# Batch 2 alone in the first MLP, its heads with values side by side, and two steps planned later

## The chip, the cores and the metric

One core of a Trainium2 chip runs the whole program in one launch. The metric is the device time of one execution in microseconds, from several timed runs; one more execution was profiled. TensorE does the matmuls, VectorE and ScalarE the elementwise work, GpSimd a little of it, and SyncE starts most of the transfers. The profile calls them PE, DVE, ACT, POOL and SP, and weight loads of TensorE PEld.

## The reference

Three stages run one behind the other on 4 batches of 448 tokens, all in float32 (weights come as float64):

```
attn = softmax(cap * tanh(q @ k.T / (8 * cap))) @ v     # 12 heads of 64, 448 tokens, per batch
x    = attn, heads side by side                         # (448, 768) per batch
xn   = (x - mean) / sqrt(var + 1e-6) * g_ln
x    = x + relu(xn @ w_ch1) @ w_ch2                     # first MLP, hidden 3072
u    = x + (relu(x.T @ w_tok1) @ w_tok2).T              # tokens mixed, hidden 256
out  = u + relu(u @ w_ch1') @ w_ch2'                    # second MLP, hidden 1536
```

## The kernel before

Activations lie transposed: 768 channels as 6 blocks of 128 partitions, 448 tokens along the free axis. A product of the MLPs is split in high and low parts of float32 and takes three passes (high by high, low by high, high by low), so a hidden block is 18 matmuls of 448 columns (L587) and an output block, over a group of four hidden blocks, 12 (L608). The first MLP has 6 such groups, the second 3. Each group is 4 + 6 weight tiles; a tile is converted from float64 the first time (`piece`, L269, on ScalarE and VectorE), stored split in DRAM (`kept`), and loaded from there in every later use (L296). There are three tile buffers (`split`).

The batches are staged. Batches 0 and 1 do their attention first, in early heads with float32 matmuls (L363, L384). Batch 0 then does one group of the first MLP alone, batches 0 and 1 do five groups as a pair (each tile serves both), batch 1 makes up its first group while batch 0 mixes tokens, and so on through the second MLP. Batches 2 and 3 follow in the same manner. Their heads are laid into the stream of the first two batches: scores from split operands (L366), tanh and exp on ScalarE (L369, L370), maxima on VectorE (L374), the split of the exponentials (L394, L396 to L400), and the values.

There are two ways to do the values of such a head. The usual one (L411 to L414) keeps 96 + 64 weight columns, the high part of v with 32 columns of ones beside it, which give the sums, and the low part. It takes 11 matmuls for a head, and the last block of tokens uses 64 rows for one of them. The other, for batches in `BESIDE` (L62, L406 to L409), puts high and low part of v side by side in 128 columns: 7 matmuls for a head, but no sums. VectorE then sums the exponentials itself (L421, two instructions of 896 columns), adds two small instructions (L425, L426), and the two halves of the result are joined through ScalarE (L429) and VectorE (L430).

Nothing is issued in the order of the code. `add` records steps with a key, their engines, and what they read and write. `emit` (L121) then plays the steps through a model with a cost for each engine and a shared port of VectorE and GpSimd ("+" in an engine's name), takes of the steps that are ready the one with the lowest key, and writes the instructions in that order. Each engine executes its own queue in order. Steps of heads and norms on TensorE get a key lowered by `URGENT` (1000), so they go as soon as the model has them ready. The keys come from numbers such as `T_ATT2` and `PACE2` (L68): batch 2's heads start at key 171.18, one for every 25.

`N_AHEAD` groups of weights are converted ahead of the first MLP, beside the early heads (L717). `normalise` (L534) takes a buffer of its own for each of six blocks (`centred`, of which four are the buffers `own` for the heads' exponentials).

Of the kernel before, what the change touches and what calls it, by code (L numbers as in the profile page):

```python
# [15 lines left out]
ALU = mybir.AluOpType  # L16
# [42 lines left out]

URGENT, SCORES, PREPARE, LOAD = 1000.0, 19.31, 4.58, 24.58  # L60

BESIDE = (3,)  # L62

N0, N1, N20, N2 = 1, 3, 1, 2
T_LN0, T_LN1 = 7.69, -20.0
T_AHEAD, N_AHEAD, AHEAD_PACE = 14.0, 1, 5.0
T_ALONE, STRETCH0, T_PAIR, STRETCH1 = 85.0, 1.3, 165.0, 1.14
T_ATT2, PACE2, T_ATT3, PACE3 = 171.18, 25.0, 500.0, 40.0  # L68
LEAD, RAW_AHEAD, EVACUATE, TOKENS_AHEAD = 6.3, 9.57, -7.49, 17.25


# [15 lines left out]
class Program:  # L87
# [33 lines left out]
    def emit(self):  # L121
# [10 lines left out]
        for _ in self.steps:  # L132
            t, e = min((max(free[e], min(s.ready for s in q)), e) for e, q in queue.items() if q)
            step = min((s for s in queue[e] if s.ready <= t), key=lambda s: s.key)
            for other in step.engines:
                queue[other].remove(step)
            step.run(e) if step.flexible else step.run()
            if e in step.port:
                t = port = max(t, port) + step.engines[e]
            else:  # L140
                t += step.engines[e]
            free[e] = end = t
            end += self.LATER.get(e, 0.0)
            for s in step.users:
                s.ready = max(s.ready, end + (0.2 if e not in s.engines else 0.0 if e == "pe" else 0.13))
                s.waits -= 1
                if not s.waits:
                    enter(s)
# [3 lines left out]
def block_kernel(ctx: ExitStack, tc: tile.TileContext, qkv, cap, gln, w1, w2, wt1, wt2, con, out):  # L152
# [111 lines left out]


    raws, wholes = ring(RAW), ring(WHOLE)
    kept = {}

    def piece(src, m, target, to):  # L269

# [6 lines left out]
        add("act", m, lambda: act(lo, lo.bitcast(U32), AF.Copy, scale=2.0 ** -29), (), [r])  # L277
        add("dve+", m // 2, lambda: dve.tensor_scalar(f, f, 3, None, op0=ALU.logical_shift_left), (), [w])  # L278
        add("dve+", m, lambda: dve.scalar_tensor_tensor(f, hi, -(1 << 31), f, op0=ALU.bitwise_and, op1=ALU.bitwise_or), [r], [w])  # L279
        add("dve+", m, lambda: dve.tensor_tensor(f, f, lo, op=ALU.add), [r], [w])  # L280
        g = f.bitcast(F32)
        add("act/dve*+", m, lambda e: copy(e, target[:, 0], g), [w], to)
        add("dve+", m, lambda e: low(engine_of[e], target[:, 1], g, target[:, 0]), [w], to)

    def load(no, w, row, cols):

# [247 lines left out]
    def normalise(b):  # L534
        rstd = RSTD[0]
        eng = LN_ENGINES[b]
        for e in range(NCC):
            o, g = centred[e], BIG[b % 2][e]
            if b >= 2:
                subtract(b, e, o)  # L540
            add("dve+", S, lambda o=o, e=e: dve.scalar_tensor_tensor(
# [172 lines left out]
    with tc.manual_schedule():  # L714
        setup()
        prog.key = T_AHEAD
        for g in range(N_AHEAD):  # L717
            prepare(g)
        prog.key = 0.0
        attention(0, 0.0, 3.97)  # L720
        prog.key += T_LN0
# [75 lines left out]
```

## Time and profile before

| | |
|---|---|
| median of 3 runs | 1398.46 us (1396.95 to 1399.26) |
| profiled execution | 1399.07 us, span 1397.3 us |
| TensorE busy | 1370.9 us, 98% of the span, 6512 matmuls |
| VectorE busy | 887.7 us, 64% |
| ScalarE busy | 612.0 us, 44% |
| GpSimd busy | 63.2 us, 5% |
| chain that ended last | PE 89%, DVE 6%, ACT 3%, DMA 1% |
| mean granted clock of TensorE | 0.995 |

A row of the windows has, behind the stretch and its length, the busy time of PE, PEld, DVE, ACT and POOL with their instructions in brackets, then the granted clock, the mean share of the transfer engines, and GB/s. A row of a timeline has start and time of an instruction or of several alike; the end of a matmul is modelled, and matmuls overlap, so the step from one start to the next tells what one costs. The times of one engine's instructions can overlap a little too. In the order of instructions below, a row is one instruction of an engine's queue, or several alike (x3), with what it writes and reads.

### The profile page before, as it was taken

Reading aid. Unit: us, or ns where it says so; the run is one execution under the profiler, and the core shown is the slowest. Engines: PE = TensorE matmul, PEld = TensorE weight load, DVE = VectorE, ACT = ScalarE, POOL = GpSimd, SP = SyncE. Lnnn points to the kernel's source line nnn. Section 1 sums busy time; section 2 is a strip of 40 time slices with the busy share of each in tenths; the row PEclk is TensorE's granted clock in tenths of the full one; section 3 lists DMA queues with packets and bytes.
Section 4 is the critical chain, followed back from the end, with each engine's and each line's share of the span. In section 5 each row is a group of like instructions: output and inputs, shape, how many; then the busy total and the mean of one; then the engine's idle time right before and its main releaser. Section 6 shows DMA issues by size and latency. Waiting matters only on the chain.

```text
span 1397.3 us, 17773 instructions
## 1 busy us (share of the span) xinstructions
PE 1370.9 (98%) x6512; PEld 1178.4 (84%) x6512; DVE 887.7 (64%) x1602; ACT 612.0 (44%) x995; POOL 63.2 (5%) x52
## 2 busy tenths in 40 slices
PE   8999989999999999999999999999999999999998
PEld 3335578889898999988999999999999999999997
DVE  5999698988898899999989973212122232232221
ACT  7986567675657656776656421010100111111000
POOL 0000002010011001100010000000000000000000
PEclk9999999999999999999999999999999999999999
DMA  8885447667675756467565576643232456554366
GB/s 264 275 268 161 142 123 244 226 203 227 196 229 191 240 177 223 156 218 235 192 202 195 178 232 200 208 149 128 84 122 93 148 166 189 186 168 151 124 197 194
DMA packets 135671, 262.16 MB, mean 188 GB/s; under 512 B 10144, under 2 KB 72864, under 8 KB 135584
## 3 DMA queue, kind: packets, MB, share of 16 engines
q1 hardware_dynamic: 135008, 260.74, 57.9%
q8 instruction: 51, 0.84, 0.2%
q10 hardware_dynamic: 576, 0.29, 0.1%
q14 instruction: 36, 0.29, 0.1%
HBM read 198.86 MB, written 62.13 MB: 187 GB/s over the span
## 4 chain that ended last, share of the span: by engine, by line
PE 89%; DVE 6%; ACT 3%; DMA 1%; issue 1%; SPq 0%; ACTq 0%; DVEq 0%
PE bank L587 37%; PE bank L608 37%; PE sc L366 3%; PE bank L384 3%; PE bank L682 2%; PE bank L663 2%; PE bank L408 1%; PE sc L363 1%; DVE m L374 1%; ACT x L369 1%; PE bank L414 1%; PE bank L413 1%; PE bank L466 1%; ACT x L370 1%; PE bank L639 1%
## 5 line engine op out<-in xcount | busy, mean ns | idle before, releaser
L608 PE MATMUL bank<-h,split 128*128 128x448 f32 x2592 | 547.9, 367 | 3.4 <-DVE x L612 2.9
L587 PE MATMUL bank<-big,split 128*128 128x448 f32 x2592 | 548.1, 368 | 3.0 <-ACT big L543 2.0
L587 PEld LDWEIGHTS bank<-big,split 128*128 128x128 f32 x2592 | 485.9, 188 | 48.2 <-ACT big L543 3.3
L608 PEld LDWEIGHTS bank<-h,split 128*128 128x128 f32 x2592 | 484.9, 188 | 46.7 <-DVE x L612 3.6
L592 ACT ACTIVATE h<-bank 128x448 fp32r<-128x448 f32 x144 | 78.3, 544 | 398.1 <-PE bank L587 397.6
L612 DVE TENSOR_TENSOR x<-x,bank 128x448 f32<-128x448 f32 x216 | 133.4, 619 | 186.1 <-PE bank L608 184.0
L593 DVE SCALAR_TENSOR_TENSOR h<-bank,h 128x448 fp32r<-128x448 f32 x144 | 89.3, 621 | 183.9 <-ACT h L592 183.3
L276 ACT ACTIVATE whole<-raw 128x384 f32<-128x384 f32 (+2 forms) x130 | 77.6, 600 | 45.4 <-DVE split L172 42.0
L280 DVE CUSTOM_DVE_ANT_0 whole<-raw,whole 128x768 uint16<-128x768 uint16 (+2 forms) x130 | 85.6, 659 | 0.6
L172 DVE TENSOR_TENSOR split<-whole,split 128x384 fp32r<-128x384 f32 (+1 forms) x126 | 79.2, 632 | 4.3 <-ACT split L176 3.6
L279 DVE SCALAR_TENSOR_TENSOR whole<-raw,whole 128x384 int32<-128x384 int32 (+2 forms) x130 | 81.3, 627 | 0.2
L277 ACT ACTIVATE raw<-raw 128x384 int32<-128x384 uint32 (+2 forms) x130 | 77.6, 600 | 0.0
L176 ACT ACTIVATE split<-whole 128x384 fp32r<-128x384 f32 (+1 forms) x85 | 47.9, 564 | 43.6 <-PE bank L608 19.7
L172 POOL TENSOR_TENSOR ks<-area,ks 64x512 fp32r<-64x512 f32 x23 | 31.7, 1377 | 675.5 <-ACT ks L347 675.5
L374 DVE TRANSPOSE_TENSOR_REDUCE m<-x 128x28 f32<-128x896 f32 x48 | 52.5, 1101 | 8.2 <-ACT x L370 7.7
L278 DVE TENSOR_SCALAR whole<-whole 128x384 int32<-128x384 int32 (+2 forms) x130 | 53.7, 416 | 2.3 <-ACT whole L276 1.9
L374 DVE TRANSPOSE_TENSOR_REDUCE m<-area 128x28 f32<-128x896 f32 x48 | 52.9, 1102 | 0.8 <-ACT area L370 0.8
L369 ACT ACTIVATE area<-sc,tsc 128x896 f32<-128x896 f32 x48 | 48.2, 1005 | 11.1 <-DVE el L400 6.3
L370 ACT ACTIVATE area<-area,cap_t 128x896 f32<-128x896 f32 x48 | 49.9, 1040 | 0.6
L369 ACT ACTIVATE x<-sc,tsc 128x896 f32<-128x896 f32 x48 | 46.7, 996 | 6.9 <-DVE tsc L252 4.3
L394 ACT ACTIVATE eh<-area 128x896 fp32r<-128x896 f32 x48 | 45.4, 946 | 9.4 <-PE bank L408 3.5
L370 ACT ACTIVATE x<-x,cap_t 128x896 f32<-128x896 f32 x48 | 49.0, 1037 | 0.3
(117 smaller groups left out, 1116.0 us busy)
## 6 DMA issues: line engine op xcount, KB each, us to landing
split<-kept SPq DMA_DIRECT2D x136, 384.0 KB, 4.1
split<-kept SPq DMA_DIRECT2D x102, 512.0 KB, 3.7
raw<-in_w SPq DMA_DIRECT2D x72, 384.0 KB, 3.5
kept<-split SPq DMA_DIRECT2D x72, 384.0 KB, 3.6
raw<-in_w SPq DMA_DIRECT2D x54, 512.0 KB, 4.0
kept<-split SPq DMA_DIRECT2D x54, 512.0 KB, 3.3
area<-in_qkv SPq DMA_DIRECT2D x38, 480.0 KB, 4.1
area<-in_qkv SPq DMA_DIRECT2D x35, 192.0 KB, 3.3
```

The lines of the kernel that those rows point to most:

```text
L172: eng.tensor_tensor(out, whole, high.bitcast(F32), op=ALU.subtract)
L276: add("act", m, lambda: act(f.bitcast(F32), hi.bitcast(F32), AF.Copy, scale=2.0 ** -112), [r], [w])
L279: add("dve+", m, lambda: dve.scalar_tensor_tensor(f, hi, -(1 << 31), f, op0=ALU.bitwise_and, op1=ALU.bitwise_or), [r], [w])
L280: add("dve+", m, lambda: dve.tensor_tensor(f, f, lo, op=ALU.add), [r], [w])
L369: add("act", 2 * S, lambda e=e, sc=sc: act(e, sc.at[:, :, :S], AF.Tanh, scale=tsc), [sc], eb)
L370: add("act", 2 * S, lambda e=e: act(e, e, AF.Exp, scale=cap_t), (), eb)
L374: add("dve", 2 * S, lambda half=half, e=e: dve.tensor_reduce(m.at[:, half].rearrange("p c j -> p (c j)"), e.rearrange("p c (j i) -> p (c j ...
L587: mm(ph.at[:, :S], w[:, wi, cc * P:(cc + 1) * P], src[cc].at[:, xi], start=(cc, n) == (0, 0), stop=(cc, n) == (NCC - 1, 2))
L592: add("act", S, lambda ht=ht, ph=ph: act(ht.at[:, 0], ph.at[:, :S], AF.Relu), [ph], [ht], early=EVACUATE)
L593: add("dve", S, lambda ht=ht, ph=ph: dve.scalar_tensor_tensor(ht.at[:, 1], ph.at[:, :S], 0.0, ht.at[:, 0].bitcast(F32), op0=ALU.max, op1=A ...
L608: mm(py.at[:, :S], w[:, wi, i * P:(i + 1) * P], h[i].at[:, hi], start=(i, n) == (0, 0), stop=(i, n) == (G - 1, 2))
L612: add("dve", S, lambda x=x, py=py: dve.tensor_tensor(x.at, x.at, py.at[:, :S], op=ALU.add), [py], [x], early=EVACUATE)
```

## The change

`BESIDE` holds batch 2 as well. N1 goes from 3 to 6: batch 2 does all six groups of the first MLP alone, and batch 3 all six alone, beside batch 2's token mixing and behind it; the pair of the two shares only the second MLP. The keys of the heads of batches 2 and 3 are other numbers. In `emit`, a TensorE step with a key below zero (a step of a head or a norm) that reads what another engine wrote is planned 2.0 us later than the model has its input, past 200 us of the model's time. In the group converted ahead, the integer addition and the low part of the split go to GpSimd. `normalise` uses the two buffers `two` in turn for batches 2 and 3.

```diff
-BESIDE = (3,)
-
-N0, N1, N20, N2 = 1, 3, 1, 2
+BESIDE = (2, 3)
+SPARE, SPARE_FROM = 2.0, 200.0
+
+N0, N1, N20, N2 = 1, 6, 1, 2
-T_ATT2, PACE2, T_ATT3, PACE3 = 171.18, 25.0, 500.0, 40.0
+T_ATT2, PACE2, T_ATT3, PACE3 = 230.0, 35.0, 650.0, 25.0
...
             for s in step.users:
-                s.ready = max(s.ready, end + (0.2 if e not in s.engines else 0.0 if e == "pe" else 0.13))
+
+                spare = SPARE if "pe" in s.engines and s.key[0] < 0 and end > SPARE_FROM else 0.0
+                s.ready = max(s.ready, end + (0.2 + spare if e not in s.engines else 0.0 if e == "pe" else 0.13))
...
-    kept = {}
+    kept, ahead = {}, False
...
-        add("dve+", m, lambda: dve.tensor_tensor(f, f, lo, op=ALU.add), [r], [w])
+        add("pool+" if ahead else "dve+", m, lambda e: engine_of[e].tensor_tensor(f, f, lo, op=ALU.add), [r], [w])
...
-        add("dve+", m, lambda e: low(engine_of[e], target[:, 1], g, target[:, 0]), [w], to)
+        add("pool+" if ahead else "dve+", m, lambda e: low(engine_of[e], target[:, 1], g, target[:, 0]), [w], to)
...
-            o, g = centred[e], BIG[b % 2][e]
+            o, g = centred[e] if b < 2 else two[e % 2], BIG[b % 2][e]
...
         prog.key = T_AHEAD
+        ahead = True
         for g in range(N_AHEAD):
             prepare(g)
+        ahead = False
```

The lines of the changed kernel stand three further down in the heads and the MLPs (L411 of the order now is L408 before, L590 is L587, L611 is L608, L534 is L531).

On TensorE, the first head of batch 2 in the kernel before, just behind the second norm (bank_111 takes the head's values, eh, el and vs are its split exponentials and values):

```order
```

The lines of the changed kernel stand three further down in the heads and the MLPs (L411 of the order now is L408 before, L590 is L587, L611 is L608, L534 is L531).

On TensorE, the first half of the first head's values of batch 2 in the kernel before, just behind the second norm (bank_111 takes the head's values; eh, el and vs are its split exponentials and values):

```order
L587 MATMUL bank_112<-big_84,split_77 128x448 x12
L411 MATMUL bank_111<-eh_98,vs_97 96x448
L413 MATMUL bank_111<-eh_98,vs_97 64x448
L414 MATMUL bank_111<-el_99,vs_97 96x448
L411 MATMUL bank_111<-eh_98,vs_97 96x448
L413 MATMUL bank_111<-eh_98,vs_97 64x448
L414 MATMUL bank_111<-el_99,vs_97 96x448
L587 MATMUL bank_112<-big_84,split_77 128x448 x6
```

The same half in the changed kernel:

```order
L590 MATMUL bank_114<-big_85,split_79 128x448 x18
L411 MATMUL bank_111<-eh_98,vs_97 128x448
L411 MATMUL bank_111<-el_99,vs_97 128x448
L411 MATMUL bank_111<-eh_98,vs_97 128x448
L411 MATMUL bank_111<-el_99,vs_97 128x448
L611 MATMUL bank_112<-h_86,split_77 128x448 x3
```

Six matmuls of 96 and 64 columns have become four of 128; of the second half, five have become three. The first of them stands 132 matmuls of products behind the norm's L531, where it stood 30 behind it.

On TensorE, behind the variance of batch 1's norm in the kernel before (L511 the variances, L531 the spread of the factors, big_84 and big_85 the normed input of batches 0 and 1):

```order
L511 MATMUL bank_112<-inv_c,area 112x2 x4
L587 MATMUL bank_113<-big_84,split_79 128x448 x18
L531 MATMUL bank_111<-area,ones 128x448
L587 MATMUL bank_114<-big_85,split_79 128x448 x12
L366 MATMUL sc_115<-qs_95,ks_96 128x448 x4
L587 MATMUL bank_114<-big_85,split_79 128x448 x6
L366 MATMUL sc_116<-qs_95,ks_96 128x448 x4
```

The same place in the changed kernel (L514 is L511, L369 is L366):

```order
L514 MATMUL bank_112<-inv_c,area 112x2 x4
L611 MATMUL bank_114<-h_86,split_78 128x448 x3
L611 MATMUL bank_114<-h_87,split_78 128x448 x3
L611 MATMUL bank_114<-h_88,split_78 128x448 x3
L611 MATMUL bank_114<-h_89,split_78 128x448 x3
L590 MATMUL bank_113<-big_84,split_79 128x448 x12
L534 MATMUL bank_111<-area,ones 128x448
L590 MATMUL bank_113<-big_84,split_79 128x448 x6
L590 MATMUL bank_114<-big_85,split_79 128x448 x12
L369 MATMUL sc_115<-qs_95,ks_96 128x448 x4
L590 MATMUL bank_112<-big_84,split_77 128x448 x12
L590 MATMUL bank_114<-big_85,split_79 128x448 x6
```

An output block of 12 matmuls more stands between the variances and the factors, and 6 of the 18 matmuls on batch 0 now stand behind the factors, ahead of the first on batch 1; further products on batch 0 (bank_112) come forward between those of batch 1.

On VectorE, the first pieces of weights in the kernel before (L374 and L377 are maxima of heads, L433 sums; whole and raw are a piece in conversion, split its result):

```order
L278 TENSOR_SCALAR whole_75<-whole_75 128x384
L279 SCALAR_TENSOR_TENSOR whole_75<-raw_72,whole_75 128x384
L280 ISA whole_75<-raw_72,whole_75 128x768
L374 TENSOR_REDUCE m_100<-x_82 128x28
L433 TENSOR_REDUCE rs_103<-bank_112 32x14
L172 TENSOR_TENSOR split_77<-whole_75,split_77 128x384
L278 TENSOR_SCALAR whole_76<-whole_76 128x384
L374 TENSOR_REDUCE m_100<-x_82 128x28
L279 SCALAR_TENSOR_TENSOR whole_76<-raw_73,whole_76 128x384
L377 TENSOR_REDUCE rm_105<-m_100 128x14
L280 ISA whole_76<-raw_73,whole_76 128x768
L178 CAST split_77<-whole_76 128x384
```

And GpSimd in the changed kernel, where it now has them (L283 is the addition of L280, L175 the low part of L172):

```order
L283 TENSOR_TENSOR whole_75<-whole_75,raw_72 128x384
L175 TENSOR_TENSOR split_77<-whole_75,split_77 128x384
L283 TENSOR_TENSOR whole_76<-whole_76,raw_73 128x384
L175 TENSOR_TENSOR split_77<-whole_76,split_77 128x384
L283 TENSOR_TENSOR whole_75<-whole_75,raw_74 128x384
L283 TENSOR_TENSOR whole_76<-whole_76,raw_72 128x384
L175 TENSOR_TENSOR split_78<-whole_75,split_78 128x384
L175 TENSOR_TENSOR split_78<-whole_76,split_78 128x384
```

Each piece gives an L280 and an L172 to GpSimd, 28 instructions for the 14 pieces of the group; L278, L279 and most copies (L178) stay on VectorE. ScalarE keeps the same two conversions for each piece.

## Rows read from the trace of the kernel before

**Rows 1.** windows: stretch, length, busy us (count) per engine, clock, DMA share, GB/s

```profile
18.00:90.00 72.00, 66.60 (x218) 26.88 (x217) 69.32 (x128) 70.91 (x100) 0.00 (x0) 1.00 0.89 284
90.00:131.00 41.00, 37.98 (x135) 19.09 (x133) 38.11 (x72) 31.59 (x45) 0.00 (x0) 0.93 0.59 187
175.00:200.00 25.00, 20.93 (x91) 16.92 (x90) 23.60 (x52) 15.15 (x27) 0.00 (x0) 0.93 0.28 91
200.00:490.00 290.00, 290.00 (x1411) 258.28 (x1411) 259.86 (x466) 196.49 (x326) 37.05 (x26) 1.00 0.68 218
595.00:665.00 70.00, 65.55 (x332) 59.72 (x331) 66.01 (x129) 47.77 (x90) 4.96 (x4) 0.98 0.68 223
```

**Rows 2.** timeline of TensorE: start, us, line, names; values of a batch 2 head

```profile
296.60 0.36 PE L411 MATMUL bank<-eh,vs 128*96 128x448 f32 x1
...
297.81 0.98 PE L366 MATMUL sc<-qs,ks 128*128 128x448 f32 x4
...
302.27 0.36 PE L411 MATMUL bank<-eh,vs 128*96 128x448 f32 x1
...
303.59 0.77 PE L366 MATMUL sc<-qs,ks 128*128 128x448 f32 x3
```

**Rows 3.** timeline of TensorE: values of a batch 3 head

```profile
681.84 0.36 PE L408 MATMUL bank<-eh,vs 128*128 128x448 f32 x1
...
682.65 1.38 PE L587 MATMUL bank<-big,split 128*128 128x448 f32 x6
...
689.54 0.36 PE L408 MATMUL bank<-eh,vs 128*128 128x448 f32 x1
...
690.15 2.01 PE L587 MATMUL bank<-big,split 128*128 128x448 f32 x9
```

**Rows 4.** groups by line, VectorE, 0 to 122 us: busy, mean ns, idle before

```profile
L280 DVE CUSTOM_DVE_ANT_0 whole<-raw,whole 128x768 uint16<-128x768 uint16 x8 | 4.5, 560 | 0.2
...
L172 DVE TENSOR_TENSOR split<-whole,split 128x384 fp32r<-128x384 f32 x8 | 4.2, 541 | 0.1
L172 DVE TENSOR_TENSOR split<-whole,split 128x512 fp32r<-128x512 f32 x6 | 4.1, 682 | 0.1
...
L280 DVE CUSTOM_DVE_ANT_0 whole<-raw,whole 128x1024 uint16<-128x1024 uint16 x6 | 3.9, 650 | 0.0
```

**Rows 5.** timeline of all engines, 226.5 to 230 us

```profile
227.32 1.87 POOL L172 TENSOR_TENSOR ks<-area,ks 64x512 fp32r<-64x512 f32 x1 [8.31 <-ACT ks L347]
...
227.95 1.79 DVE L280 CUSTOM_DVE_ANT_0 whole<-raw,whole 128x1024 uint16<-128x1024 uint16 x1
```

**Rows 6.** timeline of TensorE behind the second norm

```profile
188.85 0.92 PE L531 MATMUL bank<-area,ones 112*128 112x448 f32 x2
191.74 4.22 PE L587 MATMUL bank<-big,split 128*128 128x448 f32 x11 [1.96 <-ACT big L543]
```

**Rows 7.** waits of TensorE, 200 to 1397 us: us, times, longest

```profile
PE bank L682 <- DVE h L669: 2.1, 1, 2.1
PE bank L608 <- DVE x L612: 1.6, 1, 1.6
PE bank L682 <- ACT h L668: 0.6, 1, 0.6
PE bank L608 <- DMA split<-kept: 0.6, 1, 0.6
PE bank L682 <- DVE h L644: 0.2, 1, 0.2
```

**Rows 8.** groups by line, VectorE, 200 to 800 us

```profile
L374 DVE TRANSPOSE_TENSOR_REDUCE m<-area 128x28 f32<-128x896 f32 x47 | 51.8, 1102 | 0.8 <-ACT area L370 0.8
...
L421 DVE TRANSPOSE_TENSOR_REDUCE n<-area 128x28 f32<-128x896 f32 x24 | 26.3, 1097 | 0.0
```

**Rows 9.** chain of waits: start, us, what

```profile
857.78 14.60 PE bank L587 x72
...
1348.29 14.88 PE bank L608 x72
```

## The prediction

> **What bounds the kernel now.** I read the windows by stage first, then TensorE's timeline at the places that the change touches, then its waits, and last the groups of VectorE. From 200 to 490 us TensorE is busy 290.00 of 290 us at clock 1.00 [rows 1], and that is the picture up to the end but for a few waits: all of them after 200 us make 5.1 us together [rows 7]. So past 200 us the time is the number of matmuls by the step from one to the next, and only fewer or shorter matmuls, or new waits, change it. Before 131 us it is otherwise. Between 18 and 90 us ScalarE is busy 70.91 of 72 us, VectorE 69.32 and TensorE 66.60 [rows 1]: three engines nearly full at once, so relief of one alone is worth little. Two things to keep in mind: none of these waits is a head's step (those are L363 to L414), and VectorE is busy 259.86 of 290 us in the stretch from 200 to 490, 0.90 of it, without costing TensorE anything.
>
> **Values side by side (batch 2).** The row of a start to the row behind the step tells what a half of the values costs. Before, the first half goes from 296.60 to 297.81, 1.21 us for six matmuls, and the second from 302.27 to 303.59, 1.32 us for five, the one of 64 rows being slow to come and to leave [rows 2]. A head of batch 3, which has them side by side already, takes 681.84 to 682.65, 0.81 us, and 689.54 to 690.15, 0.61 us [rows 3]. So 2.53 becomes 1.42: 1.11 us a head, by 12 heads 13.3 us, all of it on an engine that never waits there. Bounds: 13 to 13.6, if the places of the heads make the step behind the 64 rows cheaper or dearer. Term: -13.3.
>
> **What the sums cost VectorE.** Each head gains two L421 of 1.097 us [rows 8], 2.2 us, 26 us over 12 heads; the other exchanges are about even. Against that the new keys spread the heads: from its first scores to its last gathering step (L444) batch 2 lay across 1206 matmuls of products and now lies across 1668. The old 1206 with 12 heads is 1206 x 0.203 + 12 x 4.15 (values and eight scores) = 295 us of TensorE, about the stretch of rows 1, with 264 us of VectorE by its share. The same products now hold 8.7 heads: 1206 x 0.203 + 8.7 x 3.04 = 271 us of TensorE. VectorE gets 8.7 x 2.2 = 19 us more and 3.3 heads less. A head's VectorE work is at least its two L374 of 1.10 us [rows 8]; with the split of the exponentials and values I estimate 6. That leaves 263 us (276 with the lower number), so VectorE would stand at 0.97 (1.02) where it stood at 0.90. Before, 0.90 cost nothing, and the stretch 595 to 665 with 66.01 of 70, 0.94, cost 4.45 us of TensorE [rows 1], though there the tokens wait on VectorE at once. With the main banks to spare I take +3 us, ends 0 and +17 (that rate, 4.45/70, over all 271 us).
>
> **The group converted ahead.** 14 pieces give two VectorE instructions each to GpSimd: 8 x 0.560 + 6 x 0.650 for L280 and 8 x 0.541 + 6 x 0.682 for L172 [rows 4], 16.8 us off VectorE before 90 us. ScalarE loses nothing and is as full; what it has free is 1.1 us up to 90 and 9.4 of the 41 us up to 131. GpSimd's own queue is empty there, 0.00 us busy [rows 1], so nothing of a head stands behind the new work, but GpSimd also holds up VectorE: an L280 that began beside a GpSimd instruction of 1.87 us took 1.79 us and ended just behind it [rows 5], against a mean of 0.650 [rows 4], so a meeting costs up to 1.14 us. Of 128 VectorE instructions in that window 28 go; of the 100 left some 42 (L278, L279, the copies) read as these do. 28 x 0.42 x 1.14 is 13 us given back, and about 3 of relief stay. Ends: 28 x 1.14 = 32 given back, a start 15 us later; none given back, and ScalarE's room, 8 us earlier. I take -3.
>
> The Trainium skill has a rule for this place (SBUF — State Buffer, Who interferes with whom): a VectorE instruction with two SBUF inputs and a GpSimd instruction that reads SBUF take one shared port for the whole instruction, and the second waits. The trace agrees, 1.79 us instead of 0.650 [rows 4, 5]; taken as a full meeting at each of the 28 it would be the later end above, and the second rival goes half the way there.
>
> **Behind the second norm.** The step that spreads the factors starts at 188.85, the next product at 191.74, 1.96 us of it idle for the normed input, and then 11 products take 4.22 us where 2.2 would do [rows 6]; the window's clock is 0.93 [rows 1], so part of the products ran at the lower of the two levels, 1.2 GHz, after that pause. Now 12 more matmuls stand ahead of L531 and six behind it that need nothing new: 1.2 us of the pause is filled for certain, and if it is short enough the clock stays and about 2 us more come back; the first values of a head no longer press in there either. I take -3, between -5 (all of it) and +2 (batch 0's products are spent earlier and are missing later).
>
> **The pace of the products.** 72 products take 14.60 us at 857.78 and 14.88 us at 1348.29 [rows 9], at the same clock: 202.8 and 206.7 ns, two steady paces. In rows 3 the nine behind a second half of side-by-side values run at the slower one (2.01 us are eight steps and a last one of 0.36: 206 each), the six behind a first half at the faster (1.38 us, 204). So side by side in batch 2 should put more products on the slow pace, and batch 3's three groups behind the tokens of batch 2 are at a place like that of 1348.29, where the pair ran like 857.78. I count some 700 products more at 3.9 ns: +2.7 us, ends 0 and +6.
>
> **Edits at nothing.** N1 = 6 leaves the matmuls as they are. It adds 42 loads (24 of 384 KB, 18 of 512 KB), all of kept tiles: a group alone needs 6.3 MB in 29 us, 215 GB/s, with a head's 0.7 MB every 20 us 250; 284 GB/s ran between 18 and 90 us [rows 1]. They go through SyncE's queue behind the same buffers as now; without that cover each late tile would cost 0.6 us, as the one of the weight loads did [rows 7]. Planning heads 2 us later removes no wait, since none there is a head's [rows 7]; it puts the step behind some ten products, and a head has 28 us of TensorE until the next, so its cost is 0, ends -1 and +1. The two norm buffers make each block wait for the one before last, some six times 2.5 us of serial work that VectorE's queue carries among the evacuations behind it (L612), under a group of batch 1's products (144 x 0.203 = 29 us). Mixing tokens of batches 0 and 1 loses the heads beside it, but VectorE gets batch 2's norm there: 0, ends -4 and +4.
>
> **Sum.** -13.3 + 3 - 3 - 3 + 2.7 = -13.6 us on 1399.07, the profiled execution's own time (span 1397.3 and 1.8 around it), gives 1385.5. The median shown is 0.6 us lower, so I say 1385 us.
>
> **Rivals.**
> A, VectorE becomes the bound under batch 2's heads, L612 and L593 come late and TensorE waits for banks. For it: 0.97 by my sum, with everything after it late. Against it: 0.90 to 0.93 cost nothing. It decides from a share of 1.0 on; at the rate of 595 to 665 it is +17, the start and the second norm then give nothing, since what they give is waited for again: -13.3 + 17 + 2.7 = +6.4, 1405 us. Slower.
> B, GpSimd gives back more than it takes and the second norm keeps its pause: start +4 (17 us lost to meetings and 4 more of latency, against 16.8), norm 0, VectorE +3, pace +2.7: -3.6, 1395 us. For it rows 5; against it the many instructions of that stretch that read PSUM or one input and don't meet.
> C, VectorE was the true bound of the first 131 us. Then the start gives 8, the norm 5, and no new wait comes: -13.3 - 8 - 5 + 1 = -25, 1373 us. Against it ScalarE's 70.91 of 72.
> That the change does not do what it says can only be so for the 2 us of spare: with no wait to remove it is idle in every case here.
>
> **How the numbers follow.** The forecast 0.72 (its own range 1379 to 1391), A 0.06, B 0.12, C 0.10. A measurement of this kernel tells 0.2%, 2.8 us, from no change. The forecast, C and most of B are faster by more: 0.92. Within it: 0.04, from B's far end and the near side of A. Slower: 0.04. The range 1376 to 1394 leaves out A, the larger part of C and some of B, less than 2 in 10.
>
> **What would show it.** In the profile after: values of batch 2 as seven L411 of 0.20 us a step, 48 matmuls fewer; TensorE's first main product (L590) some 3 us earlier than L587 had it, and VectorE no longer full between 18 and 90 us; after the second norm a pause under 1 us and a clock of 1.00; VectorE at 0.95 or more from 200 to 490 and short waits on L615 or L596, 3 us in all; products at 14.88 us for 72 in batch 3's last groups alone. I am wrong if TensorE's waits past 200 us pass 15 us, if the first product comes no earlier, or if a head of batch 2 still costs over 2 us of values.

## The result, and the profile after

The changed kernel takes 1381.51 us (median of 4 runs, 1379.37 to 1381.71) against 1398.28 for the kernel before: a ratio of 0.9877, interval 0.986 to 0.9894, 16.8 us faster. I had said 1385, with 1376 to 1394 around it. The profiled execution is one of 1379.37 us with a span of 1377.5, 19.8 below that of before, and the terms below are compared with those 19.8. TensorE has 6464 matmuls, 48 fewer.

The same stretches as in [rows 1]:

```profile
18.00:90.00 72.00, 66.69 (x210) 27.51 (x209) 60.40 (x100) 69.82 (x98) 32.59 (x28) 0.95 0.86 281
90.00:131.00 41.00, 38.23 (x142) 18.35 (x141) 39.74 (x78) 33.18 (x47) 0.00 (x0) 1.00 0.65 202
175.00:200.00 25.00, 21.61 (x105) 18.33 (x104) 23.70 (x56) 15.08 (x30) 0.00 (x0) 1.00 0.38 126
200.00:490.00 290.00, 290.00 (x1428) 267.46 (x1427) 262.31 (x488) 183.26 (x312) 25.29 (x18) 1.00 0.70 226
595.00:665.00 70.00, 69.67 (x346) 62.80 (x345) 65.36 (x136) 39.67 (x73) 0.00 (x0) 1.00 0.59 193
```

VectorE is relieved up to 90 us, as said; from 200 to 490 it stands at 262.31 of 290, 0.905, not at the 0.97 that I had worked out; and the stretch from 595 to 665 has got back 4 of its 4.45 idle us.

The values of a head of batch 2 on TensorE's timeline, where [rows 2] stood:

```profile
284.37 0.36 PE L411 MATMUL bank<-eh,vs 128*128 128x448 f32 x1
...
285.18 0.98 PE L369 MATMUL sc<-qs,ks 128*128 128x448 f32 x4
...
292.07 0.36 PE L411 MATMUL bank<-eh,vs 128*128 128x448 f32 x1
292.27 0.57 PE L411 MATMUL bank<-el,vs 128*128 128x448 f32 x2
292.68 7.59 PE L611 MATMUL bank<-h,split 128*128 128x448 f32 x36
```

0.81 and 0.61 us a half, just as in [rows 3]: 1.42 where 2.53 was. Behind the second norm, where [rows 6] stood:

```profile
186.55 0.92 PE L534 MATMUL bank<-area,ones 112*128 112x448 f32 x2
186.95 1.72 PE L590 MATMUL bank<-big,split 128*128 128x448 f32 x6
189.82 0.68 PE L590 MATMUL bank<-big,split 128*128 128x448 f32 x2 [1.14 <-ACT big L546]
191.14 2.31 PE L590 MATMUL bank<-big,split 128*128 128x448 f32 x10 [0.65 <-DVE big L175]
```

Six products lie in the pause, no later one runs at half speed, and the clock is 1.00. All waits of TensorE from 200 us to the end, where [rows 7] had 5.1 us:

```profile
PE bank L685 <- ACT h L671: 0.6, 1, 0.6
PE bank L611 <- DMA split<-kept: 0.4, 2, 0.2
PE bank L685 <- DVE h L672: 0.2, 1, 0.2
```

And the pace of [rows 9], from the chain of waits:

```profile
924.06 14.59 PE bank L590 x72
...
1088.58 14.88 PE bank L590 x72
```

To see where time goes I add the steps from one matmul's start to the next by the kind of the earlier one, from the 171st main product to the last matmul. A product's step counts 0.20266 us; what regular steps have above that is "pace", longer ones "stalls". All in us, for the profiled executions of eight kernels; the short names, e1 to e14, stand at the experiments below:

```
                  before   after  e1_be~  e4_old  e8_key  e9_den  e11_n1  e14_th
171st product at  195.19  192.46  194.97  194.03  191.09  194.61  192.20  193.55
products' pace      6.34    8.05   10.31    9.34    8.07    8.17    5.94    7.26
products' stalls    8.57    6.22   15.29   12.58    6.71   12.29    8.15   13.41
scores             38.40   37.64   41.27   38.27   37.66   38.46   37.60   39.31
values             47.51   34.16   38.78   44.43   48.54   36.45   34.19   45.87
tokens             72.63   70.37   71.15   71.03   71.31   75.24   70.42   70.34
norms               3.04    3.05    3.05    3.05    3.50    3.39   18.72    3.05
```

Before against after: values -13.35, stalls -2.35, tokens -2.26, scores -0.76, pace +1.71, the start with the second norm -2.73; with -0.08 for the rest that is -19.8.

### The profile page after: what moved, and what is told of

Read it like the earlier page. It is cut to its first block, busy times and chain, and to the rows that moved or that the text cites. A ratio compares the mean times of both kernels' runs of the same rounds, so it can differ in the third digit from the quotient of the medians.

```text
span 1377.5 us, 17810 instructions
## 1 busy us (share of the span) xinstructions
PE 1355.0 (98%) x6464; PEld 1171.9 (85%) x6464; DVE 892.9 (65%) x1613; ACT 619.1 (45%) x1004; POOL 97.0 (7%) x80
## 4 chain that ended last, share of the span: by engine, by line
PE 90%; DVE 4%; ACT 4%; DMA 1%; issue 1%; ACTq 0%
PE bank L590 38%; PE bank L611 37%; PE sc L369 3%; PE bank L387 3%; PE bank L411 2%; PE bank L685 2%; PE bank L666 2%; ACT x L372 1%; PE sc L366 1%; ACT x L373 1%; DVE m L377 1%; PE bank L642 1%; DMA split<-kept 1%; PE bank L469 1%; ACT whole L279 0%
## 5 line engine op out<-in xcount | busy, mean ns | idle before, releaser
L611 PE MATMUL bank<-h,split 128*128 128x448 f32 x2592 | 550.2, 367 | 1.6 <-DVE x L615 1.3
L590 PE MATMUL bank<-big,split 128*128 128x448 f32 x2592 | 548.3, 368 | 3.5 <-ACT big L546 1.8
L590 PEld LDWEIGHTS bank<-big,split 128*128 128x128 f32 x2592 | 484.8, 188 | 49.8 <-ACT big L546 2.9
L611 PEld LDWEIGHTS bank<-h,split 128*128 128x128 f32 x2592 | 485.0, 188 | 45.7 <-issue 2.5
L615 DVE TENSOR_TENSOR x<-x,bank 128x448 f32<-128x448 f32 x216 | 133.4, 618 | 162.0 <-PE bank L611 160.1
L596 DVE SCALAR_TENSOR_TENSOR h<-bank,h 128x448 fp32r<-128x448 f32 x144 | 89.3, 621 | 163.5 <-ACT h L595 163.0
L279 ACT ACTIVATE whole<-raw 128x384 f32<-128x384 f32 (+2 forms) x130 | 77.7, 601 | 46.0 <-DVE split L175 37.6
L175 POOL TENSOR_TENSOR ks<-area,ks 64x512 fp32r<-64x512 f32 x23 | 33.6, 1460 | 686.4 <-ACT ks L350 666.2
L280 ACT ACTIVATE raw<-raw 128x384 int32<-128x384 uint32 (+2 forms) x130 | 77.4, 599 | 0.1
L283 DVE CUSTOM_DVE_ANT_0 whole<-raw,whole 128x768 uint16<-128x768 uint16 (+2 forms) x116 | 74.2, 642 | 0.1
L179 ACT ACTIVATE split<-whole 128x384 fp32r<-128x384 f32 (+1 forms) x92 | 51.9, 566 | 43.8 <-PE bank L611 29.6
L175 DVE TENSOR_TENSOR split<-whole,split 128x384 fp32r<-128x384 f32 (+1 forms) x112 | 69.4, 622 | 2.1 <-ACT split L179 1.8
L377 DVE TRANSPOSE_TENSOR_REDUCE m<-x 128x28 f32<-128x896 f32 x48 | 52.7, 1103 | 10.5 <-ACT x L373 10.0
L377 DVE TRANSPOSE_TENSOR_REDUCE m<-area 128x28 f32<-128x896 f32 x48 | 52.9, 1102 | 6.6 <-ACT area L373 6.6
L424 DVE TRANSPOSE_TENSOR_REDUCE n<-area 128x28 f32<-128x896 f32 x48 | 52.8, 1099 | 0.1
```

The costliest lines, as they stand in the source:

```text
L175: eng.tensor_tensor(out, whole, high.bitcast(F32), op=ALU.subtract)
L279: add("act", m, lambda: act(f.bitcast(F32), hi.bitcast(F32), AF.Copy, scale=2.0 ** -112), [r], [w])
L283: add("pool+" if ahead else "dve+", m, lambda e: engine_of[e].tensor_tensor(f, f, lo, op=ALU.add), [r], [w])
L377: add("dve", 2 * S, lambda half=half, e=e: dve.tensor_reduce(m.at[:, half].rearrange("p c j -> p (c j)"), e.rearrange("p c (j i) -> p (c j ...
L590: mm(ph.at[:, :S], w[:, wi, cc * P:(cc + 1) * P], src[cc].at[:, xi], start=(cc, n) == (0, 0), stop=(cc, n) == (NCC - 1, 2))
L596: add("dve", S, lambda ht=ht, ph=ph: dve.scalar_tensor_tensor(ht.at[:, 1], ph.at[:, :S], 0.0, ht.at[:, 0].bitcast(F32), op0=ALU.max, op1=A ...
```

## The experiments

They are told by question, not in the order of running. Each is timed against the kernel before, run beside it on the same chip.

**Which edit carries the gain?** Values alone (e1):

```diff
-BESIDE = (3,)
+BESIDE = (2, 3)
```

> The kernel before with only the values of batch 2 side by side (old keys, N1 = 3, no group converted ahead on GpSimd, no spare, one buffer for the norm). Theory 1 (the parts add): the 48 matmuls that go and the step behind the 64 rows are worth 13.3 us wherever the heads lie, so about 1385 us against 1398, a ratio of 0.990 to 0.992, with VectorE's share under batch 2's heads below 1 and TensorE's waits past 200 us as before, some 5 us. Theory 2 (the values need the new keys): with the old, denser keys VectorE gets 26 us more on 264 in about 282 us, a share of 1.03, TensorE waits for banks there, and the gain shrinks to 5 us or less: 1393 us or more, with new waits on VectorE between 200 and 490 us.

1400.67 us, ratio 1.001 (0.9997 to 1.0023). Theory 1 falls. Theory 2's time holds, though VectorE's share from 200 to 490 us is 0.947 (274.62 of 290) and not 1.03: the largest term of my sum, alone, gives nothing. The longest waits of TensorE from 200 us on, two of the three for ScalarE:

```profile
PE sc L366 <- ACT area L369: 3.8, 4, 2.4
PE bank L608 <- DVE x L612: 3.5, 5, 1.1
PE bank L608 <- ACT raw L277: 2.1, 1, 2.1
```

By the account above the values fell by 8.7 instead of 13.4, scores, stalls and pace took 13.6 (2.9, 6.7 and 4.0). The pace's part lies behind 840 us, where batch 2's heads are long over: the chain of waits has 72 products at 886.24 us in 14.88 us, at a place where [rows 9] have 14.60. The keys and N1 alone, with the old values (e8):

```diff
-N0, N1, N20, N2 = 1, 3, 1, 2
+N0, N1, N20, N2 = 1, 6, 1, 2
-T_ATT2, PACE2, T_ATT3, PACE3 = 171.18, 25.0, 500.0, 40.0
+T_ATT2, PACE2, T_ATT3, PACE3 = 230.0, 35.0, 650.0, 25.0
```

> The kernel before with the new keys alone (N1 = 6, T_ATT2 230, PACE2 35, T_ATT3 650, PACE3 25), the values of batch 2 still one behind the other. Theory 1 (side-by-side values and denser or sparser heads work against each other on VectorE: the old keys are right for the old values and stop 15 us of TensorE with the new ones): the new keys alone bring only the tokens' stall back, 3 to 5 us: 1393 to 1396 us. Theory 2 (the keys are worth 15 us by themselves, and the values add nothing): 1382 to 1385 us. Theory 3 (the keys alone cost): 1400 us or more.

1396.45 us, ratio 0.9988 (0.9977 to 0.9998): 1.7 us, below theory 1's 3 to 5 and far from theory 2. So neither half is worth more than 2 us by itself. Now from the other side, the changed kernel with both sets of numbers back (e4):

```diff
-N0, N1, N20, N2 = 1, 6, 1, 2
+N0, N1, N20, N2 = 1, 3, 1, 2
-T_ATT2, PACE2, T_ATT3, PACE3 = 230.0, 35.0, 650.0, 25.0
+T_ATT2, PACE2, T_ATT3, PACE3 = 171.18, 25.0, 500.0, 40.0
```

> The changed kernel with the old keys of the heads (batches 2 and 3) and N1 = 3 put back; values side by side, the group converted ahead on GpSimd, the spare time and the norm's two buffers stay. Theory 1 (the keys bring the tokens' waits down and cost a little of the pace): the stall of 4 to 5 us of the tokens around 600 us comes back, the pause behind the second norm too (2 to 3 us at most), the slow pace is shorter (1 to 2 us less): about 1381.5 + 4.6 + 1 - 1.5 = 1386 us. Theory 2 (VectorE decides as soon as batch 2's heads lie dense): share 1.03 in their stretch, 1393 us or more. Theory 3 (the keys are worth nothing): 1381 to 1383.

1398.98 us, ratio 1.0002 (0.9991 to 1.0013): all is lost. That is far more than theory 1's 4.6; it lies within theory 2's 1393 or more, but VectorE's share from 200 to 490 us is 0.924, not 1.03. The largest single wait stands behind the first values of batch 2; TensorE's timeline:

```profile
202.54 0.37 PE L411 MATMUL bank<-el,vs 128*128 128x448 f32 x1
209.35 2.61 PE L590 MATMUL bank<-big,split 128*128 128x448 f32 x6 [6.44 <-DVE h L596]
```

The product waits for a bank that VectorE empties (L596). VectorE's queue from 202 to 209 us holds without a gap the sums and split of that first head, conversions of the next weights, and two of the split's instructions stretched to 1.58 us beside GpSimd's; the L596 begins at 208.69:

```profile
201.66 1.07 DVE L424 TRANSPOSE_TENSOR_REDUCE n<-area 128x28 f32<-128x896 f32 x1
...
204.75 1.58 DVE L175 TENSOR_TENSOR el<-area,eh 128x448 fp32r<-128x448 f32 x1
...
206.72 1.58 DVE L403 SCALAR_TENSOR_TENSOR el<-eh,kc,area 128x448 fp32r<-128x448 f32 x1
...
208.69 1.14 DVE L596 SCALAR_TENSOR_TENSOR h<-bank,h 128x448 fp32r<-128x448 f32 x2
```

The distance of batch 2's heads alone (e9):

```diff
-T_ATT2, PACE2, T_ATT3, PACE3 = 230.0, 35.0, 650.0, 25.0
+T_ATT2, PACE2, T_ATT3, PACE3 = 230.0, 25.0, 650.0, 25.0
```

> The changed kernel with batch 2's heads planned 25 us apart again instead of 35 (PACE2), everything else as changed: first key 230, N1 = 6. Theory 1 (the distance of the heads is what keeps VectorE's queue short enough for the evacuations): TensorE's products wait behind L411 and for L596 and L615 again, 8 to 15 us more, 1389 to 1396 us. Theory 2 (the place, first key 230 with batch 2 alone in the first MLP, decides): waits at most 2 us more, 1380 to 1384 us.

1394.81 us, ratio 0.9968 (0.9955 to 0.9981), 13.3 us above the changed kernel, the size that theory 1 had. But VectorE's share from 200 to 490 us is only 0.913 (264.73 of 290): not the mean load but single clashes cost, most of all two waits of products for L615, here the larger one (TensorE's timeline):

```profile
618.25 4.07 PE L611 MATMUL bank<-h,split 128*128 128x448 f32 x10 [3.38 <-DVE x L615]
```

The ten products behind it take 4.07 us, about twice the usual (the granted clock is 0.73 from 612 to 623 us): the pause costs its length and then half-speed steps. What stood ahead of that L615 on VectorE:

```profile
613.31 1.79 DVE L282 SCALAR_TENSOR_TENSOR whole<-raw,whole 128x512 int32<-128x512 int32 x1
615.03 1.34 DVE L281 TENSOR_SCALAR whole<-whole 128x512 int32<-128x512 int32 x1
...
617.50 0.61 DVE L615 TENSOR_TENSOR x<-x,bank 128x448 f32<-128x448 f32 x1
```

These are two conversions of weights, long because GpSimd works beside them (1.72 us from 612.84 and 1.45 from 614.63), and no step of a batch 2 head, whose last scores are at 496 us. By the steps above their regular length, some 10 of about 16 us that this execution loses lie between 500 and 700 us, beside the tokens. So the distance is worth 13.3 us, but that it works by a short queue under the heads is shown for the smaller part at most; the rest is what the other plan puts beside the tokens. N1 alone, which I had priced at nothing (e11):

```diff
-N0, N1, N20, N2 = 1, 6, 1, 2
+N0, N1, N20, N2 = 1, 3, 1, 2
```

> The changed kernel with N1 = 3: the first MLP's batch 2 together with batch 1 from the third group on, as before, the heads' new keys kept. Theory 1 (the heads' distance decides, N1 only where the products lie): 1381 to 1385 us, VectorE's share from 200 to 490 us near 0.9. Theory 2 (the group alone is needed: without it the second norm's products and the tokens fall together): the pause behind the second norm and the tokens' stall back, 1387 us or more.

1397.05 us, ratio 0.9993 (0.9984 to 1.0003): 15.5 us lost, a time that theory 2 allows, but by neither theory's mechanism: the second norm's pause (1.14 and 0.65 us) and the tokens are as in the changed kernel (tokens 70.42). Nearly the whole loss is at one place, the last batch's norm (18.72 us of steps where 3.05 were):

```profile
897.68 1.78 PE L590 MATMUL bank<-big,split 128*128 128x448 f32 x8
899.30 0.91 PE L498 MATMUL bank<-area,inv_c 128*128 128x448 f32 x2
908.10 1.66 PE L514 MATMUL bank<-inv_c,area 128*112 128x2 f32 x8 [7.88 <-DVE area L509]
912.67 1.86 PE L534 MATMUL bank<-area,ones 112*128 112x448 f32 x2 [2.92 <-DVE area L531]
916.50 1.86 PE L590 MATMUL bank<-big,split 128*128 128x448 f32 x4 [1.96 <-ACT big L546]
```

Between these steps there is no product: those that don't need this norm are used up at 899 us. Counted in main products, the norm's first step stands behind 3060 of them here, its last one behind 3060 too; in the changed kernel behind 3066 and 3150. So N1 = 6 is what leaves 84 products to lie inside the last norm. Then these three parts together, without GpSimd's group, the spare time and the norm's two buffers (e14):

```diff
-BESIDE = (3,)
+BESIDE = (2, 3)
-N0, N1, N20, N2 = 1, 3, 1, 2
+N0, N1, N20, N2 = 1, 6, 1, 2
-T_ATT2, PACE2, T_ATT3, PACE3 = 171.18, 25.0, 500.0, 40.0
+T_ATT2, PACE2, T_ATT3, PACE3 = 230.0, 35.0, 650.0, 25.0
```

> The kernel before with three parts of the change alone: values of batch 2 side by side, N1 = 6, and the heads' new keys. No group converted ahead on GpSimd, no spare time, one buffer for the norm. Theory 1 (these three carry the gain together, each without the others giving at most 4 us): 1380 to 1385 us. Theory 2 (the start and the second norm need GpSimd's share and the norm's buffers): 1386 to 1390 us, with the pause behind the second norm as before and VectorE full from 18 to 90 us.

1401.58 us, ratio 1.0025 (1.0016 to 1.0034). Both theories fall. Up to 772 us this kernel is far ahead: its product 2500 starts at 772.11, against 796.06 with the old values (e8). Then it loses 30 us in 76: product 2700 starts at 848.17 against 842.26. TensorE there:

```profile
805.74 0.57 PE L408 MATMUL bank<-el,vs 128*128 128x448 f32 x2
808.28 0.74 PE L408 MATMUL bank<-eh,vs 128*128 128x448 f32 x1 [1.97 <-ACT eh L394]
...
810.98 3.36 PE L366 MATMUL sc<-qs,ks 128*128 128x448 f32 x8
814.13 0.58 PE L408 MATMUL bank<-eh,vs 128*128 128x448 f32 x1
814.50 0.87 PE L408 MATMUL bank<-el,vs 128*128 128x448 f32 x2
817.62 0.44 PE L408 MATMUL bank<-eh,vs 128*128 128x448 f32 x1 [2.25 <-DVE vs L172]
...
822.79 3.07 PE L587 MATMUL bank<-big,split 128*128 128x448 f32 x6 [2.77 <-ACT big L543]
```

For 17 us nothing but the steps of the last heads, one after the other, 7.9 us of it waits for ScalarE or VectorE; then six products that had to wait for a normed block, at half speed (3.07 us; the mean granted clock from 780 to 840 us is 0.86). VectorE shows why the blocks are late; then the same step in the changed kernel:

```profile
818.40 1.10 DVE L421 TRANSPOSE_TENSOR_REDUCE n<-area 128x28 f32<-128x896 f32 x1
...
820.42 1.11 DVE L484 TENSOR_TENSOR area<-x,mean 128x448 f32<-128x448 f32 x2
821.46 1.27 DVE L541 SCALAR_TENSOR_TENSOR area<-area,gl,rstd 128x448 f32<-128x448 f32 x2
...
825.01 1.10 DVE L421 TRANSPOSE_TENSOR_REDUCE n<-area 128x28 f32<-128x896 f32 x1
...
828.30 1.16 DVE L484 TENSOR_TENSOR area<-x,mean 128x448 f32<-128x448 f32 x2
829.38 1.28 DVE L541 SCALAR_TENSOR_TENSOR area<-area,gl,rstd 128x448 f32<-128x448 f32 x2
```

```profile
748.78 0.68 DVE L544 SCALAR_TENSOR_TENSOR area<-area,gl,rstd 128x448 f32<-128x448 f32 x1
...
754.03 1.27 DVE L544 SCALAR_TENSOR_TENSOR area<-area,gl,rstd 128x448 f32<-128x448 f32 x2
...
759.89 0.63 DVE L544 SCALAR_TENSOR_TENSOR area<-area,gl,rstd 128x448 f32<-128x448 f32 x1
```

Four of the six blocks of batch 2's norm are worked in `centred[2]` to `centred[5]`, the four tiles of `own`, and a late head keeps its exponentials in the same tiles. So two blocks come right behind the last sum of one half (818.40), two behind that of the other (825.01), when batch 3's heads are over; with the two other buffers all six are done by 761 us, and the last heads then lie among batch 2's products (last values at 876 us, here at 826). Before, the blocks are late as well (792 to 804 us), but its dearer values had left products for that long. The two buffers, priced at nothing, thus free batch 2's products as filler for the last heads: of the steps above their regular length 20.3 us lie between 780 and 870 us here, and none in the changed kernel. The buffers were not run alone: that they and not GpSimd's group together with the spare bring the 20 us rests on these rows, and on the next two runs, in which each of the other two is missing.

**GpSimd's group and the spare.** The group first (e2):

```diff
-        ahead = True
+        ahead = False
```

> The changed kernel with the group that is converted ahead back on VectorE instead of GpSimd. Theory 1 (the first main product came 2 us earlier in the changed kernel, of which 1 us was left behind batch 0's and 1's attention): 1382 to 1383.5 us, the first product at 122 us and VectorE at 69 of 72 us between 18 and 90 us. Theory 2 (GpSimd's share also decides the pause behind the second norm): 1385 us or more.

1381.34 us, ratio 0.9885 (0.9871 to 0.9898): no difference from the changed kernel. Its first product starts at 122.47 (120.25 there), and the pause behind the second norm is back whole: 1.96 us before two products, then 0.44, 0.60 and 0.45. The 171st product is 1.8 us later, the end 1.9, which the medians don't show. So GpSimd's group, not N1, moves products into that pause (e8, with N1 = 6 and without the group, has it whole too), and what the group gives is worth 2 us at most. The clock isn't decided there: it stays at 1.00 from 175 to 200 us here, behind the same 1.96 us that [rows 6] have with half-speed products behind them; e11 has the six products in the pause and still 0.93.

The spare (e3):

```diff
-SPARE, SPARE_FROM = 2.0, 200.0
+SPARE, SPARE_FROM = 0.0, 200.0
```

> The changed kernel with the 2 us of spare for steps on TensorE behind heads and norms set to 0. Theory 1 (idle: no wait of before past 200 us was a head's): the same as the changed kernel within 0.2%, 1380 to 1383 us, waits of heads' steps on TensorE at most 1 us in all. Theory 2 (the spare is what keeps the heads' steps from waiting now that VectorE has 26 us more): waits of 0.2 to 0.5 us at each of the 36 late heads' steps, 3 to 8 us, 1385 us or more.

1378.29 us (1375.27 to 1381.13), ratio 0.9859 (0.9841 to 0.9877): not worse. Theory 1's mechanism holds, for TensorE's only wait past 200 us is one of 0.5 us for a tile of weights; the time lies 1.7 us below its range, and whether the kernel is 3 us better, these runs don't settle.

**Does VectorE pay for the sums?** The sums alone, in the kernel before (e12):

```diff
+            if b == 2 and not early:
+                spare = next(sums)
+                for half in range(2):
+                    e, eb = E[half]
+                    add("dve", 2 * S, lambda half=half, e=e: dve.tensor_reduce(
...
```

> The kernel before with two sums over a head's exponentials added for each of batch 2's 12 heads on VectorE (1.10 us each, 26 us in all), into a tile that nobody reads; its values stay one behind the other, its keys are the old ones. Theory 1 (what the side-by-side values lose with the old keys is paid for these sums: VectorE cannot take them in where the heads lie 25 us apart): the 13 us that go missing with side-by-side values appear here as a loss, 1406 us or more, with TensorE waiting for L593 and L612 between 200 and 640 us. Theory 2 (26 us more of VectorE cost 4 us at most, as the doubled sums did with the new keys; what is lost is TensorE's own, since its products come sooner to the same evacuations): at most 1403 us.

1405.56 us, ratio 1.0058 (1.0042 to 1.0074), 7.7 us slower: between the theories, nearer the first. That these 7.7 us are all the sums', and 7.7 of the 13 that go missing in e1, is not shown: of the 10.2 us that its profiled execution (1409.25 us) is longer than that of before, 4.8 are the pace, again mostly behind 840 us, and some 5 are left for the sums. The same load with the new keys (e7):

```diff
+                    if b == 2:
+                        add("dve", 0, lambda half=half, e=e: dve.tensor_reduce(
...
```

> The changed kernel with batch 2's two sums over a head's exponentials (L424, 1.10 us each) issued twice, to the same result: 24 more VectorE instructions, 26 us, in the stretch whose VectorE share is 0.90. Theory 1 (waits begin well below a share of 1, as the old keys with side-by-side values showed at 0.92 and 0.95): the share goes to 0.97 or more, TensorE waits 8 to 20 us, 1390 to 1400 us. Theory 2 (VectorE costs only from a share of 1.0 on): waits of at most 3 us, 1381 to 1384 us.

1385.53 us, ratio 0.991 (0.9891 to 0.9928), 4.0 us more than the changed kernel: between the theories again. Under batch 2's heads it costs nothing:

```profile
200.00:490.00 290.00, 290.00 (x1430) 267.56 (x1429) 276.24 (x497) 184.93 (x313) 25.57 (x18) 1.00 0.70 225
```

At 0.953 of VectorE TensorE does not wait at all, while the old plan (e4) left it 9.5 us idle there at 0.924 (268.10 of 290). What costs there is a clash that the plan makes, not the share. The 4 us arise later: 4.7 of the profiled execution's 6 lie between 500 and 700 us, beside the tokens and the norm.

**The pace.** A state or a place (e6)?

```diff
+                    if e == NCC - 1 and b >= 2:
+                        mm(pu.at[:32, S:S + 32], kc[:, :32], kc[:, :32], start=True, stop=True)
```

> The changed kernel with one short fp32 matmul (32 rows, 32 columns, into columns of PSUM that nobody reads) added behind the last token matmul of batches 2 and 3, just ahead of the main products that follow; it computes nothing that is used. Theory 1 (the pace of the products, 202.7 or 206.7 ns a step, is a state that the kind of matmul ahead of the run leaves behind, and the tokens' 384 columns leave the slow one): the 558 products from 1060 us and the 582 from 1253 us run at 202.7 instead of 206.7, 4.5 us less at a cost of some 0.5: about 1377.5 us, ratio to the changed kernel 0.997. Theory 2 (the pace belongs to the place or the data, to batch 3's rows or to what the queues do then): the same pace, 1382 us.

1378.31 us (1377.66 to 1378.95), ratio 0.986 (0.9845 to 0.9874). The chain of waits has it; the same 72 products as the last row above:

```profile
1089.80 14.60 PE bank L590 x72
...
1342.25 14.60 PE bank L590 x72
```

All 1140 products now run at 202.7 ns, and the pace's excess falls from 8.05 to 3.28 us. Theory 2 falls; theory 1's pace and time hold. That the kind of matmul ahead is what sets the pace is not shown by it (see the last section). 3.2 of the 4.8 us arrive in the median; in the profile, longer stalls and gathering steps (L469) took 2.5 back. Both harmless edits together (e10):

```diff
-SPARE, SPARE_FROM = 2.0, 200.0
+SPARE, SPARE_FROM = 0.0, 200.0
+                    if e == NCC - 1 and b >= 2:
+                        mm(pu.at[:32, S:S + 32], kc[:, :32], kc[:, :32], start=True, stop=True)
```

> The changed kernel with the short fp32 matmul behind the token matmuls of batches 2 and 3 and without the 2 us of spare, the two edits that did no harm alone. Theory 1 (the pace's 4.5 us are a gain of its own, the spare idle): products from 1060 us to the end at 202.7 ns, 1376 to 1379 us. Theory 2 (what the pace gives is waited for at the last groups' loads): new waits for split tiles behind 1250 us, 1380 us or more.

1372.28 us (1370.92 to 1375.94), ratio 0.9828 (0.9813 to 0.9843): faster than both kernels, by 25.6 and by 9.2 us, and more than the two edits alone add up to (6.4). Theory 1 has the mechanism and its bound is passed. Part of it is not the edits': the clock is 1.00 from 18 to 131 us, where without the short matmul (e3) 0.95 and 0.96 were granted to the same instructions, and the 171st product starts 4.4 us earlier (190.31 against 194.73). Its five runs agree: the three with a mean granted clock of 1.00 took 1370.92 to 1372.28 us, the two with 0.996 and 0.995 took 1375.94 and 1375.85, which is what the two edits add up to within 1 us.

## Why the prediction was right, point by point

**Values, -13.3: measured -13.35.** The size is exact. What I took for certain, "all of it on an engine that never waits there", was not: with the old keys the same 48 matmuls less give nothing (e1), because stalls and scores took 9.6 us and the pace 4.0. With the old plan and the other parts (e4) the rows show a sum and the split of a head in VectorE's queue ahead of a product's bank; for e1 itself that is argued from e12, and the pace's part lies elsewhere.

**VectorE, +3: measured 0 or less.** Stalls and scores fell by 3.1 us. Its share came out at 0.905 instead of 0.97; over the whole run it is busy 892.9 us, 5.2 more than before, where 26 us of sums less the 8.9 below would be 17. By groups over the whole run, the sums (L424) are 26.5 us more and what goes with them (L428, L429, L433, L436) 4.5, but the conversions' L283 and L175 fell by 21.3, more than the 16.8 that were moved; the rest is spread over small groups. The rate that I took for the bounds, 4.45 us in 70, was a clash of the tokens and not a price per share (e7).

**Start -3 and second norm -3: measured -2.7 together.** The first product comes 2.2 us earlier (120.25 against 122.46), and by the 171st product only 0.5 more are gained: the norm's term is the one that was mis-sized. The pause did close; the prediction named no edit for it, and e2 shows that it goes with GpSimd's group. That the clock held goes with neither: e2 has the whole pause and holds it, e11 has the pause filled as in the changed kernel and doesn't. VectorE's busy time up to 90 us fell by 8.9 of the 16.8 us that were moved, so its other instructions there took 7.9 us more; I had said 13 of at most 32. The Trainium skill's rule (SBUF — State Buffer, Who interferes with whom) that VectorE and GpSimd take the shared port in turn agrees in its sign; a full meeting at each of the 28, 32 us, is not what these rows show.

**Pace, +2.7: measured +1.7.** One of the two places was right, the groups behind the tokens of batch 2 (from 1000 to 1200 us the pace's excess is 2.6 us where 1.0 was). The other was not: behind side-by-side values 29 of 35 runs of products are at the faster pace.

**Token mixing, 0: measured -2.3.** That is inside its bounds, and the stretch of [rows 1] that lost 4.45 us now loses 0.3.

**Edits at nothing: the step that failed.** "N1 = 6 leaves the matmuls as they are" and "the two norm buffers make each block wait for the one before last": both true and beside the point. I priced each edit against the waits of the kernel before. N1, without which 15.5 us are lost (e11), the distance of 35, 13.3 us (e9), and by the rows of e14 the buffers, some 20 us, remove no wait that stood there; they prevent waits that the other parts would otherwise open. The buffers cover the cheaper values: e14 and e8 differ by these alone, and only e14 runs out of products at the last heads. N1 covers the new keys rather than the values: with N1 = 3 and the old keys (e1) the norms' steps are 3.04 us, with N1 = 3 and the new ones (e11), whose last heads end at 876 us instead of 809, they are 18.72. The distance prevents clashes on VectorE, most of them beside the tokens. The sum came out because all of these covers were made at once. Rival A's direction was nearer than the 0.06 that I gave it: without N1, without the distance, or without the buffers (and two edits worth little) the change lands within 4 us of the kernel before, though in e11 and e14 not because VectorE is full under batch 2's heads.

Against the 19.8 us of the profiled executions my 13.6 is 6.2 short: 6.1 from VectorE's term (+3 said, -3.1 measured), 2.3 from the tokens, 1.0 from the pace, less 3.3 that start and norm didn't give. That misses of both signs met is luck, and so is part of the nearness. The medians differ by 3 us less, since the profiled execution after lies 2.1 below its median and that of before 0.8 above.

## What to carry to other kernels

Where one engine is full, making its work shorter is worth its full size only as long as other work is there to fill in: count the filler that is left at the last serial steps (a norm, the last heads) after the cut, not before it. Edits that remove no wait today can be what keeps the next one away, so price a change's parts together, and leave one out at a time to learn what each is for. An average share of an engine says little about waits; look for what stands in its queue at the moment when the other engine needs one result.

## What the runs showed of the hardware that I had not expected

TensorE's 448-column products behind weight loads have two steady paces at the same granted clock of 1.00: 202.7 and 206.7 ns. A pace stays through hundreds of products, and one added fp32 matmul of 32 x 32 turned it (e6: 1140 products changed over, 4.8 us for an insert of 0.36). Behind the tokens' 384-column matmuls (L666) all 12 runs of six or more products in the changed kernel are at the slow pace. Behind the other kinds both occur: 27 of 30 runs are fast behind the transposes of 128 columns (L642), 6 of 12 behind the tokens' 448-column matmuls (L685), where the longest runs start. So the kind of the matmul just ahead doesn't settle it. The same products, behind the same matmuls in the same order, in the changed kernel and in e6, some 400 us ahead of its insert:

```profile
618.98 29.03 PE L590 MATMUL bank<-big,split 128*128 128x448 f32 x138
```

```profile
619.07 28.46 PE L590 MATMUL bank<-big,split 128*128 128x448 f32 x138
```

The first runs at 206.7 ns, the second at 202.6. What sets the pace stays open. The Trainium skill (TensorE: Matmul & The Clock Gate, Wait — 56ns, not 53.3ns?) gives matmuls back to back a step of N / 2.4 GHz and some 2.5 ns once warm, which would be 189 ns for 448 columns by my estimate; neither of the two paces agrees, and the measurement decides.

A pause of 2 to 4 us can cost a second time, by half-speed products behind it, and need not. Behind the 3.38 us of e9 ten products took 4.07 us, and behind the 2.77 us of e14 six took 3.07, against 0.203 each; behind 1.96 us eleven took 4.22 in [rows 6] at a granted clock of 0.93, while in e2 the products behind the same 1.96 us kept a clock of 1.00.
